# New tables of order, PSUM banks and engines for a fused attention and phase-mixer kernel

## The chip, the cores and the metric

The kernel runs on one core of one Trainium2 chip. The metric is the device time of one execution in microseconds (us), the median of several runs. A core has five engines with a queue each, and each runs its queue in order: PE (TensorE, matrix products), DVE (VectorE), ACT (ScalarE), POOL (GpSimd) and SP (SyncE, which here only issues DMA transfers). Work of one engine that needs another's waits on a semaphore, and everything behind it in that engine's queue waits too.

## The reference

```
def _attn_ref(q, k, v):                       # (8, 8, 576, 64) each
    scores = scale * np.matmul(q, k.transpose(0, 1, 3, 2))
    mask = block_i >= block_j                 # causal, in blocks of 64
    scores = np.where(mask, scores, -1000000000.0)
    attn = softmax(scores)
    return np.matmul(attn, v)

def _moe_ref(x, w_theta, w_tok_r, w_tok_i, w_ch):   # x: (8, 576, 512)
    theta = x @ w_theta
    zr, zi = x * np.cos(theta), x * np.sin(theta)
    y = einsum('ts,bsd->btd', w_tok_r, zr) + einsum('ts,bsd->btd', w_tok_i, zi)
    u = x + y
    return u + np.maximum(u @ w_ch, 0.0)

def reference(...):
    x = attention of all heads, laid out as (batch, 576, 512)
    return _moe_ref(x, ...)
```

Everything is float32. Eight batches of eight heads each go through attention; the result of a batch, 576 by 512, goes through the mixer.

## The kernel before

The work is cut into 3,404 **parts**, each a small function with a key, the parts that it needs, and where it matters a PSUM bank and an engine that are chosen for it. Heads are numbered 0 to 63 and handled in pairs 0 to 31; batch b has the pairs 4b to 4b + 3. Products in float32 accuracy are made of three float16 products (a high part times a high part and the two cross terms), which is why most tensors exist as a high and a low half.

A **pair** is loaded as `rq`, `rk`, `rv` in groups of two pairs (line 772). Its scores are made by PE into the two wide banks and two narrow ones (lines 589 and 596) and, for the first 64 rows, into a corner of the bank of the outputs (line 617). DVE takes row maxima (line 633), DVE or POOL turns them into the bias `mn` (line 641), ACT takes exponentials into `t` (line 646). The exponentials are split: the high half by a cast (`high`, line 431 on ACT, 433 on DVE or POOL), the low half by a subtraction (`low`, line 436, on DVE or POOL). SP transposes the halves by DMA (`pt<-p`, line 665), in two pieces A and B for heads below 16 and in one piece above. PE multiplies them with `v` (line 680, 45 products for a head), and DVE divides by the row sums (lines 692, 694, 698) into `xn`; a small DMA (line 686) moves one corner.

The **mixer** of a batch follows its four pairs: `xn` is split (`xh`, `xl`: lines 431/433 and 436) and transposed by DMA (`xT<-xp`, line 806); PE makes theta (lines 816 and 819), ACT and DVE make cosine and sine (828, 834, 440/442, 849, 851), DVE or POOL multiplies with x (`z`, line 860) and splits (`zh`, `zl`). PE mixes tokens with `wT` (line 884, five pieces for each of eight tiles: the **mix**), DVE makes u (893; `xs`, line 889, is the sum of x's halves), ACT/DVE/POOL splits u (423/425/427 and 900), PE mixes channels (907), ACT or DVE clips (913/915) and DVE adds up (923); SP stores (927).

The **weights** come in float64 words and are brought into two float16 halves in the first 110 us: a load (462), `exponent` on ACT (471), `lowest` (477 on ACT, 479 on POOL, 481 on DVE), `narrow` on DVE (485), `plain` (440 on ACT, 501 on DVE), a product with ones on PE for the largest size (494), `high` (423 on ACT, 425 on DVE, 427 on POOL) and `low` on DVE (507).

The scales of the values in `v` (and of q, k from the fourth batch on) also need a small product on PE (line 374) of a diagonal that POOL makes (368).

No scheduler runs when the kernel is built. What stands where is written in three **tables**: `ORDER` lists all parts in the order in which they are emitted, and so sets the order on every queue; `BANKS` gives one of the eight PSUM banks to each of 371 takings of a bank; `PLACES` gives one of A (ACT), D (DVE) and P (POOL) to each of 915 parts that could go to more than one engine. They are used in one function:

```
    keys, names, places, place = list(parts), iter(BANKS), iter(PLACES), {}
    for key in keys:
        for label in parts[key].takes:
            of_label[label] = banks[int(next(names))]
        if parts[key].on:
            place[key] = next(places, parts[key].on[0])
    done = set()
    for n in ORDER:
        key = keys[n]
        assert done.issuperset(parts[key].needs), key
        parts[key].f(*([place[key]] if parts[key].on else []))
        done.add(key)
```

Of the kernel before, what the change touches and what calls it, by code (L numbers as in the profile page):

```python
# [37 lines left out]
    8, 160, 158, 16, 9, 10, 11, 17, 18, 335, 363, 339, 364, 372, 373, 374, 340, 0, 1, 350, 351, 19, 12, 352, 353,  # L38
    375, 336, 387, 2, 334, 361, 3, 362, 365, 24, 337, 386, 32, 33, 25, 56, 338, 341, 392, 376, 342, 26, 57, 40, 58,
    41, 366, 367, 20, 27, 162, 42, 4, 343, 368, 5, 48, 59, 49, 28, 391, 390, 354, 50, 43, 163, 13, 344, 21, 29, 34,  # L40
    385, 51, 35, 369, 415, 164, 401, 60, 165, 414, 388, 345, 72, 413, 44, 104, 64, 136, 88, 96, 80, 161, 346, 347,
    105, 106, 402, 403, 412, 166, 416, 167, 168, 389, 36, 65, 73, 89, 97, 423, 169, 52, 74, 170, 171, 172, 159, 90,
    393, 66, 394, 98, 332, 81, 355, 82, 137, 107, 75, 348, 437, 395, 67, 37, 396, 397, 398, 138, 120, 424, 333, 99,
    112, 383, 45, 53, 349, 404, 377, 76, 83, 384, 139, 100, 356, 61, 14, 91, 417, 84, 418, 68, 92, 69, 357, 441, 77,
    358, 85, 425, 359, 93, 101, 465, 370, 141, 151, 466, 121, 122, 436, 113, 176, 142, 143, 178, 144, 94, 371, 114,
    115, 439, 419, 360, 78, 378, 420, 489, 440, 116, 22, 399, 438, 443, 62, 123, 6, 38, 494, 379, 464, 421, 442,
    444, 380, 173, 452, 447, 445, 434, 540, 463, 467, 446, 145, 15, 128, 140, 426, 427, 174, 381, 468, 469, 70, 405,
    406, 474, 152, 453, 108, 448, 30, 487, 31, 435, 470, 449, 454, 86, 455, 456, 180, 400, 124, 129, 130, 471, 491,
    490, 495, 407, 514, 408, 409, 410, 488, 382, 475, 428, 476, 477, 478, 545, 496, 1804, 492, 422, 450, 497, 493,
# [12 lines left out]
    650, 673, 631, 604, 669, 611, 693, 1854, 1869, 651, 670, 646, 1855, 645, 656, 657, 1864, 639, 612, 613, 698,
    614, 1857, 1865, 652, 678, 658, 632, 564, 691, 1862, 196, 1858, 1859, 692, 633, 586, 615, 1863, 626, 653, 679,
    680, 681, 694, 695, 689, 659, 699, 700, 660, 682, 654, 661, 696, 701, 1908, 697, 1909, 744, 634, 1866, 721, 674,
    702, 1910, 720, 197, 1899, 729, 1914, 1915, 730, 707, 718, 635, 1870, 191, 1867, 1916, 1900, 1873, 1901, 199,
    636, 1871, 683, 690, 703, 719, 708, 709, 1885, 637, 675, 710, 722, 200, 676, 2004, 2007, 1881, 201, 119, 655,
    662, 663, 664, 665, 711, 1911, 749, 1884, 704, 1912, 705, 712, 1880, 2005, 155, 1907, 731, 1877, 1902, 723, 684,
    1893, 1917, 724, 202, 1903, 1894, 1895, 725, 1888, 1872, 1896, 1897, 1918, 1892, 666, 1898, 1913, 677, 203,
    1904, 2008, 1889, 2006, 1882, 685, 1919, 743, 1890, 1876, 1878, 1886, 1879, 742, 686, 1874, 1875, 1905, 687,
    726, 727, 785, 195, 732, 747, 748, 745, 746, 750, 753, 204, 706, 713, 205, 1944, 765, 714, 715, 716, 754, 751,  # L70
    752, 755, 733, 1945, 756, 764, 767, 766, 157, 1938, 1887, 1883, 1939, 734, 1940, 206, 768, 688, 771, 1946, 2009,
    790, 757, 1941, 758, 772, 769, 1891, 770, 773, 193, 1947, 207, 135, 208, 1937, 192, 1948, 1949, 1942, 1943, 717,
    2010, 735, 728, 736, 737, 738, 740, 739, 741, 783, 784, 786, 826, 2023, 788, 787, 789, 791, 2024, 759, 808,
# [1103 lines left out]
```

## Time and profile before

| | us |
|---|---|
| median of three runs (673.57 to 674.95) | 674.0 |
| the profiled execution, its own time | 677.03 |
| its span, first instruction to last | 675.2 |
| PE busy | 614.8 |
| DVE busy | 586.5 |
| ACT busy | 508.3 |
| POOL busy | 374.3 |

The profile shows one execution. Its own time is 3.0 us over the median of the runs and 1.8 us over its span. Times inside it are counted from the start of the span. An engine is busy while an instruction runs on it; waiting and issuing don't count. Instructions that follow each other on one engine overlap a little at their ends, so the sum of durations is larger than the busy time.

### The profile page before, as it was taken

The page shows a single profiled execution, that of the slowest core. Times are in us where ns is not written, and L with a number is a line of the kernel's source. Part 1 is how long each engine was busy: PE and PEld are TensorE (multiplying, and loading weights), DVE is VectorE, ACT ScalarE, POOL GpSimd, SP SyncE. Part 2 cuts the span into 40 slices and gives each one's busy share as a digit, 9 for nine tenths or more (in the row PEclk, how much of TensorE's full clock was granted, in tenths as well). Part 3 has the DMA queues.
Part 4 walks back from the last instruction along what each step waited for, and adds up shares of the span by engine and source line. Part 5 has one row for each costly group of instructions (what it writes and reads, how often), then busy time and mean ns, then how long its engine had stood idle before and what let it go on. Part 6 is the DMA issues. An engine that isn't in the chain of part 4 may idle for free.

```text
span 675.2 us, 18061 instructions
## 1 busy us (share of the span) xinstructions
PE 614.8 (91%) x7374; PEld 456.1 (68%) x7374; DVE 586.5 (87%) x1162; ACT 508.3 (75%) x770; POOL 374.3 (55%) x391
## 2 busy tenths in 40 slices
PE   5376688998999999999999998999899999999997
PEld 3155545785688577775787756785677477867775
DVE  3988889998997999989998899999998999976554
ACT  5888669885987998877998799979987997225021
POOL 2463536853667467961677628744593457931530
PEclk9577788999999999999999999999999999999999
DMA  8999999899969688879789977999779547930003
GB/s 349 336 264 224 196 196 225 183 202 187 202 141 237 132 190 188 183 157 185 202 178 154 206 168 169 199 165 213 169 177 184 93 81 161 189 78 2 19 1 123
DMA packets 268515, 116.58 MB, mean 173 GB/s; under 512 B 256016, under 2 KB 256016, under 8 KB 268432
## 3 DMA queue, kind: packets, MB, share of 16 engines
q1 hardware_dynamic: 268432, 115.43, 79.1%
q8 instruction: 57, 0.93, 0.6%
q14 instruction: 26, 0.21, 0.1%
HBM read 42.01 MB, written 9.44 MB: 76 GB/s over the span
## 4 chain that ended last, share of the span: by engine, by line
PE 52%; DVE 22%; DMA 10%; ACT 8%; POOL 4%; issue 4%; SPq 1%; ACTq 0%; POOLq 0%; DVEq 0%
PE g L884 12%; PE s L884 8%; DMA pt<-p 7%; PE g L680 7%; DVE m L633 5%; PE g L816 5%; PE g L907 5%; PE s L589 4%; PE s L907 4%; DVE p L436 3%; PE s L816 3%; ACT t L646 3%; PE g L589 2%; DMA xT<-xp 2%; PE s L819 1%
## 5 line engine op out<-in xcount | busy, mean ns | idle before, releaser
L884 PEld LDWEIGHTS <-zh 128*128 128x128 f16 x1152 | 112.7, 98 | 29.8 <-issue 1.1
L884 PE MATMUL g<-wT_h,zh 128*128 128x288 f16 x405 | 115.9, 286 | 1.0 <-DVE u L893 0.8
L884 PE MATMUL g<-wT_h,zl 128*128 128x288 f16 x405 | 115.8, 286 | 0.1
L884 PE MATMUL g<-wT_l,zh 128*128 128x288 f16 x405 | 115.8, 286 | 0.0
L680 PE MATMUL g<-v,pt 128*128 128x65 f16 x2880 | 102.9, 197 | 13.3 <-DMA pt<-p 6.5
L680 PEld LDWEIGHTS <-pt 128*128 128x128 f16 x2880 | 99.0, 100 | 20.3 <-DMA pt<-p 10.3
L633 DVE TENSOR_REDUCE m<-s 128x1 f32<-128x576 f32 (+2 forms) x132 | 85.3, 672 | 6.9 <-PE s L596 6.9
L436 POOL TENSOR_TENSOR p<-t,p 128x512 f16<-128x512 f32 (+4 forms) x28 | 66.5, 2376 | 43.8 <-ACT p L431 38.9
L431 ACT CAST p<-t 128x1600 f16<-128x1600 f32 (+4 forms) x66 | 84.3, 1283 | 8.5 <-DMA pt<-p 4.4
L436 DVE TENSOR_TENSOR p<-t,p 128x1600 f16<-128x1600 f32 (+4 forms) x52 | 84.9, 1635 | 5.0 <-ACT p L431 3.5
L860 POOL TENSOR_TENSOR aa<-aa,xn 128x256 f32<-128x256 f32 (+1 forms) x59 | 48.3, 832 | 60.3 <-ACT aa L849 44.4
L816 PEld LDWEIGHTS <-xT 128*128 128x128 f16 x384 | 36.6, 99 | 46.9 <-DMA xT<-xp 4.3
L884 PEld LDWEIGHTS <-zl 128*128 128x128 f16 x576 | 56.3, 98 | 16.3 <-issue 1.6
L646 ACT ACTIVATE t<-s,m,size 128x576 f32<-128x576 f32 (+1 forms) x80 | 59.1, 778 | 7.8 <-POOL m L641 6.5
L907 PEld LDWEIGHTS <-wch_h 128*128 128x128 f16 x512 | 48.1, 98 | 15.8 <-issue 2.8
L633 DVE TENSOR_REDUCE m<-g 128x1 f32<-128x192 f32 (+2 forms) x156 | 54.4, 372 | 4.5 <-PE g L596 4.4
L646 ACT ACTIVATE t<-g,m,size 128x320 f32<-128x320 f32 (+2 forms) x100 | 49.0, 535 | 11.9 <-DVE m L641 5.7
L436 POOL TENSOR_TENSOR zl<-aa,zh 128x512 f16<-128x512 f32 (+1 forms) x36 | 40.8, 1139 | 15.3 <-ACT zh L431 9.5
L884 PE MATMUL s<-wT_h,zh 128*128 128x288 f16 x171 | 48.9, 286 | 0.0
L884 PE MATMUL s<-wT_l,zh 128*128 128x288 f16 x171 | 48.9, 286 | 0.0
L884 PE MATMUL s<-wT_h,zl 128*128 128x288 f16 x171 | 48.9, 286 | 0.0
L907 PE MATMUL g<-uh,wch_h 128*128 128x288 f16 x160 | 45.8, 286 | 1.4 <-DVE u L893 0.8
(194 smaller groups left out, 1624.3 us busy)
## 6 DMA issues: line engine op xcount, KB each, us to landing
rv<-in_v SPq DMA_DIRECT2D x16, 768.0 KB, 5.4
rq<-in_q SPq DMA_DIRECT2D x16, 640.0 KB, 5.1
rk<-in_k SPq DMA_DIRECT2D x16, 576.0 KB, 5.0
out<-xT SPq DMA_DIRECT2D x32, 288.0 KB, 2.8
w_raw<-in_w_tok SPq DMA_DIRECT2D x5, 576.0 KB, 6.7
pt<-in_w_tok SPq DMA_DIRECT2D x4, 576.0 KB, 8.5
w_raw<-in_w_theta SPq DMA_DIRECT2D x4, 512.0 KB, 7.0
w_raw<-in_w_ch SPq DMA_DIRECT2D x4, 512.0 KB, 4.7
```

The source lines that it names most:

```text
L431: nc.scalar.copy(out=out, in_=x)
L436: engine_of(on).tensor_tensor(out=out, in0=x, in1=y, op=ALU.subtract)
L589: nc.tensor.matmul(to[hh][:, col:col + n], lhsT=qq[rows, P + P * i:P + P * i + P], rhs=kk[rows, k0:k0 + n], start=nn == 0 and col % 512 == ...
L633: nc.vector.tensor_reduce(out=self.m[:, i:i + 1], in_=self.scores_of(i), axis=AX.X, op=ALU.max)
L646: nc.scalar.activation(out=t_parts[self.hh][:, to:to + n], in_=self.scores_of(i), func=AF.Exp, scale=self.scales()[0], bias=self.m[:, NI + ...
L680: nc.tensor.matmul(o[:, i, :], lhsT=source[:, block, :], rhs=vv[:, slot, hh, :], start=first, stop=last)
L816: nc.tensor.matmul(g, lhsT=xT[:, xx + i, :], rhs=ww[:, dt, :], start=first, stop=last)
L819: nc.tensor.matmul(g[half * D:half * D + D, 0:HC], lhsT=xT[:, xx + i, 0:D], rhs=ww[:, dt, half * HC:half * HC + HC], start=first, stop=last)
L860: engine_of(on).tensor_tensor(out=cd, in0=cd, in1=self.xns[dt][:, i0:i0 + ni, :], op=ALU.mult)
L884: nc.tensor.matmul(g, lhsT=zz[:, kk, cols], rhs=ww[:, kk, ts], start=(n == 0 and kk == k0 and nn == 0), stop=n == 4 and kk == k0 + ni - 1 ...
L907: nc.tensor.matmul(g[:, 0:HS], lhsT=ww[:, dt, e * P:(e + 1) * P], rhs=uu[:, dt, th * HS:(th + 1) * HS], start=dt == 0 and n == 0, stop=dt ...
```

## The change

The parts, what each does and what it needs are the same. The three tables are replaced: they were searched with ten sets of durations of the parts, and are now searched anew with twelve. 3,300 of the 3,404 places of `ORDER` hold another number, mostly since the parts around them moved by some places; 153 of 371 letters of `BANKS` and 341 of 915 of `PLACES` differ. D falls from 279 to 266, A rises from 289 to 296, P from 347 to 353.

```diff
 ORDER = [
-    8, 160, 158, 16, 9, 10, 11, 17, 18, 335, 363, 339, 364, 372, 373, 374, 340, 0, 1, 350, 351, 19, 12, 352, 353,
...
+    8, 9, 158, 10, 11, 160, 336, 335, 363, 364, 340, 339, 16, 17, 18, 19, 350, 341, 0, 1, 2, 3, 32, 33, 351, 334,
...
```

By kind, the parts that changed engines count, before and after:

| part | ACT | DVE | POOL |
|---|---|---|---|
| steps of the weights (lowest, plain, high) | 24, 31 | 15, 6 | 12, 14 |
| low half of exponentials | - | 52, 57 | 28, 23 |
| high half of exponentials | 66, 65 | 4, 7 | 10, 8 |
| high half of v | 24, 16 | 4, 3 | 4, 13 |
| z, the products with x | - | 57, 49 | 103, 111 |
| zh | 43, 53 | 11, 6 | 26, 21 |
| xs, the sum of x's halves | - | 17, 13 | 15, 19 |
| high half of k | 11, 15 | 3, 2 | 6, 3 |

Three places follow. Names are those of the buffers: `p0` and `p1` (in the second and third place `p_99` and `p_100`) hold the split exponentials of the first and the second head of a pair, `t_97` and `t_98` the exponentials, `s_` and `g_` are PSUM banks, `pt` is the transposed `p`.

The first place is the queue of SP some 25 us after the start, before:

```order
L462 DMA w_raw_127<-in_w_tok 128x1152
L462 DMA pt01_106<-in_w_tok 128x1152
L772 DMA rk_287<-in_k 128x1152
L772 DMA rq_314<-in_q 128x1280
L665 DMA_TRANSPOSE pt00_104<-p0_99 128x8x128
L665 DMA_TRANSPOSE pt00_104<-p0_99 128x18x128
L462 DMA w_raw_128<-in_w_ch 128x1024
```

And after:

```order
L462 DMA w_raw_127<-in_w_tok 128x1152
L462 DMA pt11_107<-in_w_tok 128x1152
L665 DMA_TRANSPOSE pt00_104<-p0_99 128x8x128
L772 DMA rq_292<-in_q 128x1280
L772 DMA rk_294<-in_k 128x1152
L665 DMA_TRANSPOSE pt00_104<-p0_99 128x18x128
L462 DMA w_raw_128<-in_w_ch 128x1024
```

The first transposition of head 0 moved ahead of the loads of q and k of the second two pairs.

The second place is the queue of DVE between the first maxima and the largest size of the theta weights, before:

```order
L436 TENSOR_TENSOR p_100<-t_98,p_100 128x1024
L633 TENSOR_REDUCE m<-g_113 128x1
L641 TENSOR_SCALAR m<-m 128x2
L501 TENSOR_SCALAR wT_h<-w_val 128x576
L633 TENSOR_REDUCE m<-g_113 128x1
L633 TENSOR_REDUCE m<-s_109 128x1
L633 TENSOR_REDUCE m<-s_110 128x1
L501 TENSOR_SCALAR wT_h<-w_val 128x576
L518 TENSOR_REDUCE size_theta<-g_112 128x1
```

And after:

```order
L433 CAST p_99<-t_97 128x1088
L436 TENSOR_TENSOR p_99<-t_97,p_99 128x1088
L633 TENSOR_REDUCE m<-s_110 128x1 x2
L726 TENSOR_REDUCE size<-size 128x1
L633 TENSOR_REDUCE m<-s_109 128x1 x2
L641 TENSOR_SCALAR m<-m 128x3
L641 TENSOR_SCALAR m<-m 128x2
L485 SCALAR_TENSOR_TENSOR w_val<-w_val,w_raw 128x576
L436 TENSOR_TENSOR p_100<-t_98,p_100 128x512
L518 TENSOR_REDUCE size_theta<-g_113 128x1
```

The `plain` steps of the token weights (line 501) left DVE here and went to ACT (line 440), and both halves of head 0's larger piece came to DVE.

The third place is the queue of POOL where the low halves of the heads 18 and 19 stood, before:

```order
L427 TENSOR_SCALAR v_87<-rv,size 128x12x64
L889 TENSOR_TENSOR u_2219<-xT 128x576
L436 TENSOR_TENSOR p_99<-t_97,p_99 128x1600
L433 CAST p_100<-t_98 128x1536
L436 TENSOR_TENSOR p_100<-t_98,p_100 128x1536
L860 TENSOR_TENSOR aa<-aa,xn 128x2x128
L641 TENSOR_SCALAR m<-m 128x5
```

And after, the queue of DVE at the same heads:

```order
L900 SCALAR_TENSOR_TENSOR ul<-u_1980,u_scales,uh 128x576
L633 TENSOR_REDUCE m<-g_113 128x1 x2
L633 TENSOR_REDUCE m<-g_111 128x1
L433 CAST p_100<-t_98 128x1536
L436 TENSOR_TENSOR p_100<-t_98,p_100 128x1536
L633 TENSOR_REDUCE m<-s_109 128x1
L860 TENSOR_TENSOR aa<-aa,xn 128x2x128
```

Head 19's high and low half went from POOL to DVE, as did the low halves of the heads 18 and 23; POOL got products `z` and sums `xs` of DVE's in exchange.

## Rows read from the trace of the kernel before

**Rows 1.** The page: busy us (share of the span) and instructions of each engine.

```profile
PE 614.8 (91%) x7374; PEld 456.1 (68%) x7374; DVE 586.5 (87%) x1162; ACT 508.3 (75%) x770; POOL 374.3 (55%) x391
```

**Rows 2.** Busy time by stretch: PE, PEld, DVE, ACT, POOL; granted clock, DMA, GB/s.

```profile
0.00:125.00 125.00, 84.40 (x913) 58.58 (x914) 103.77 (x223) 96.98 (x159) 59.02 (x90) 0.81 1.01 249
125.00:550.00 425.00, 409.21 (x5231) 303.84 (x5228) 394.04 (x779) 366.12 (x546) 260.42 (x253) 1.00 0.87 177
550.00:675.20 125.20, 121.20 (x1245) 93.63 (x1238) 88.70 (x162) 45.25 (x68) 54.82 (x50) 1.00 0.36 81
125.00:225.00 100.00, 97.24 (x1225) 75.00 (x1222) 89.43 (x190) 79.78 (x128) 64.59 (x61) 1.00 0.99 196
```

**Rows 3.** Whom PE waited for: us in total, times, longest us.

```profile
PE g L589 <- DMA rq<-in_q: 10.7, 2, 7.6
PE g L680 <- DMA pt<-p: 6.5, 6, 2.2
PE g L680 <- DVE xn L698: 3.8, 4, 1.4
```

**Rows 4.** The page's chain that ended last, share of the span by engine.

```profile
PE 52%; DVE 22%; DMA 10%; ACT 8%; POOL 4%; issue 4%; SPq 1%; ACTq 0%; POOLq 0%; DVEq 0%
```

**Rows 5.** Groups by form: count, busy us, mean ns of one, idle before them.

```profile
L436 DVE TENSOR_TENSOR p<-t,p 128x1536 f16<-128x1536 f32 x13 | 24.3, 1868 | 1.8 <-ACT p L431 1.8
L436 DVE TENSOR_TENSOR p<-t,p 128x512 f16<-128x512 f32 x5 | 3.6, 713 | 2.0 <-POOL p L433 1.3 <-ACT p L431 0.7
L436 DVE TENSOR_TENSOR xp<-xn,xp 128x640 f16<-128x640 f32 x13 | 10.7, 819 | 1.6 <-ACT xp L431 1.4
L436 DVE TENSOR_TENSOR zl<-rr,zh 128x512 f16<-128x512 f32 x11 | 9.4, 854 | 0.0
L860 DVE TENSOR_TENSOR rr<-rr,xn 128x256 f32<-128x256 f32 x20 | 10.2, 512 | 0.0
L889 DVE TENSOR_TENSOR u<-xT 128x576 f32<-128x576 f16 x17 | 18.3, 1075 | 0.1
L436 POOL TENSOR_TENSOR p<-t,p 128x1536 f16<-128x1536 f32 x11 | 36.6, 3328 | 21.6 <-ACT p L431 18.2 <-DVE r L692 2.9
L433 DVE CAST zh<-aa 128x256 f16<-128x256 f32 x3 | 2.6, 870 | 0.0
L481 DVE TENSOR_SCALAR w_raw<-w_raw 128x576 uint32<-128x576 uint32 x2 | 1.0, 488 | 0.0
L501 DVE TENSOR_SCALAR wT_h<-w_val 128x576 uint16<-128x576 uint16 x4 | 1.7, 446 | 0.0
L440 ACT ACTIVATE wT_h<-w_val 128x576 bf16<-128x576 f32 x5 | 3.3, 682 | 0.0
```

**Rows 6.** Order of time, SP, PE and DVE before 40 us: start us, us, what.

```profile
26.44 0.70 SPq L772 DMA_DIRECT2D rq<-in_q  x1
27.18 9.86 SPq L665 DMA_TRANSPOSE pt<-p  x2
...
36.32 2.18 PE L589 MATMUL g<-rk,rq 64*128 64x320 f32 x12 [3.17 <-DMA rq<-in_q]
...
26.57 1.94 DVE L641 TENSOR_SCALAR m<-m 128x2 f32<-128x2 f32 x1
```

**Rows 7.** Order of time, PE: products of the heads 15, 23, 44 and 50 begin.

```profile
154.76 1.43 PE L680 MATMUL g<-v,pt 128*128 128x65 f16 x41 [1.87 <-DMA pt<-p]
223.25 0.94 PE L680 MATMUL g<-v,pt 128*128 128x65 f16 x25 [0.29 <-DMA pt<-p]
425.48 1.20 PE L680 MATMUL g<-v,pt 128*128 128x65 f16 x34 [1.32 <-DMA pt<-p]
483.19 0.97 PE L680 MATMUL g<-v,pt 128*128 128x65 f16 x27 [1.37 <-DVE xn L698]
```

**Rows 8.** All instructions of a line: duration ns min/median/max, first and last start.

```profile
L860 POOL TENSOR_TENSOR rr<-rr,xn x44: 720/732/2240, 116.0 to 639.6; 128x256 f32<-128x256 f32 x44
L900 DVE SCALAR_TENSOR_TENSOR ul<-u,u_scales,uh x32: 804/812/3524, 168.4 to 660.9; 128x576 f16<-128x576 f32 x32
```

More of the change, by code (lines that the diff above doesn't have):

```diff
@@ L37 @@
 ORDER = [
[176 rows of a table removed]
[176 rows of a table added]
 ]
 BANKS = (
-    "5064556406401235601234601235401235601234501230101236401236501234601236501235601235401235601235401236501236501234"
-    "6012356012345012364012356012346012364012345012365012354012364012356012356012354012365012345256416041444565640601"
-    "5460114565666400654160425114445344454666166240165566554506655104502141064066556041425110660526466456611400541625"
-    "63463210534066451601352025430645142"
+    "6640455415101234601234501235401235401236501230101236401235601234601236501236401236501234601234501235401234501234"
@@ L220 @@
+    "5012356012354012364012346012346012345012356012356012364012356012364012346012354012365012356246515041550565440441"
+    "5460560214666650466150524616666244541656064530665500455604466101503640144155446541520126505646466544456100451342"
+    "31315450463621054620463501434154206"
 )
 PLACES = (
-    "DAAPDAADPDDPAAAADDDADADAAAPDAPPDAPDPPAAPADAAPAAPADAADAPPADPPDPDPAPPPDAPPADDPDADADDPPDADPPPAPADDPDPAPPAPAPDDDAPPA"
-    "DPAPADAPPAPPADPPDDDADPADPADPAPPDADPAPPADPAPPPADDADPDAPDPPDPADDADAPADPAPADADADDAPAAADADPAPDAAPADPADPPAPADPADAPADA"
@@ L224 @@
-    "DPADAPADDDDAPAAADADDAPPDDPADDADAPADAPDADAPAPADPADAAADADPPDPAAPADPADAAAPADPADAPAPADPADAAPPADDAPPAADADDADAAAPDDDAP"
-    "AAADADPAPAADPADDPPPDAPADPAPADAPADAPAADAAPPPPPPAPPPAPDPADDDAPDDAPPDAPDDAPDPADPPAPDADPPPDAAAADDAAAADAPAPDDAAAAADPP"
-    "PDPPPDDAPDPAPDPPPDDPPDDAPPPADPPADPDADDADAPAPDADADADAAAPAPAPDDAAADADDPPPPAPPDPPPPDPPPAPPPAPDPAPDPAPPPPDPPDPDPDAPP"
-    "PPAAAAADAAPPAPADDDDADAAPPPPDDPPDDPPDDPDPPAPPPAPPPAPPPAPPPAPPPADPAPADPDADAADDAADADPPPPPPAADADPPAPPDPPPPAPPPPDPPPP"
-    "DPAPPDAPPDADPDPDPPAPPADAPPDADAADADADAPADAPPPAADDAPPPDDPAPPPPPDPADDPPPDDAPPPAPDPAPPPDPPPAPPAPDPADAAADDADDAPPADAPA"
@@ L229 @@
-    "DAAADAPPADDPPPPDPPPPDPPPPPDDDPPPPDDDPDPDPPDDADDAPDDADDDAAADDADPPADAPDDDAADDDDDDPDPPDDDDPPDPPDDDPPAPPPADPPDDPPADP"
-    "PDPPADADPPADADAADAD"
+    "ADAAAAADPPAPAADPAAPAAPAAPAAADAADPAAAPAAADPPAPAAPAAPADDDPPDDPPPPDPDADPADDADPDDPDADPAPDAPDDPDPADPAPDAPDAPAPADPAPPA"
+    "DPPDADAPPAPPADPPDDPADPADPADPAPAPADPADDADPAPAPADDADPDADDDDPDADDADADADDADAADPADDAPAAPPADDAPAAAPADDADPPAPADPADAPADA"
+    "PPADAAAPDDPAPAAADADPAPPDPDADDADAAAPAPPADADPDPDPADAAPDADPPDPAAPADDADAAPDADDADAAPPADPPDAAPPADPAPAAAPADDADAAAPADDDP"
@@ new lines @@
+    "AAAPDDDAPAAPPAPPAPPPPPADPADDDAPADAPADDAAPDDDPPAPPPAPPDADPPDPDDAPDPADDDAPPPADPPAPPADPPDDAAAAAADADADADAPDPAAAAAPDP"
+    "PPDAPPPAPPPAPPPDDDPAPDDPDDPAPPPADPPPPPADAPAPAADDDAADAPDADAPDDDAAAAPPAPDPAPDPADDDAPPPPPDDAPPPADDPAPPDAPPPPPPPPAPP"
+    "PDDAAAADAAPPPDAPDDADADDPPAPPDAPPDPPDPAPPPAPPDAPPPAPDDPPPPADPDAPPAPPDPDADAAADDADAPAPAPAPAADDDPPADPPPPPPAPDPAPPPAP"
+    "DPAPPPAPDPAPPDADPPAPPPDADPPADDDDADADAPADAPAPAADDDPDPPPPAPPPPPDPAPPPPPPPAPDDADPPAPPPAPDPAPDADPDDPAAAADAAAAPDADDPA"
+    "DAAADAPPADPDADPPADPDADPDPPPPPDPDPPPDDPPPPPPPPPPAPADAPDADDAADADPDDPPPADDDADADPPDDDDPPPAPPPPDDPPPPPPDPPPPDDDPPDAPP"
@@ L231 @@
+    "PADPDDAPADPDADDAAAA"
 )
```

350 rows, old and new, of the table ORDER are left out of this document.

## The prediction

> **What bounds the kernel now.** I read the page's busy times first, then the busy times by stretch, then whom PE waited for, then the chain that ended last. PE is busy 614.8 us of 675.2 [rows 1], so some 60 us are idle, and the stretches say where: 125.00 − 84.40 = 40.6 us before 125, 425.00 − 409.21 = 15.8 us from 125 to 550, and 125.20 − 121.20 = 4.0 us after that [rows 2]. The reader is to see two limits. After 125 PE leaves almost nothing free, and since the matrix products are the same parts in both kernels, the tables can win there no more than parts of the 15.8 us. Before 125 PE waits for data: its largest waits of all are for the loads of q (10.7 us) [rows 3]. The chain that ended last agrees: PE 52%, DVE 22%, DMA 10%, ACT 8%, POOL 4% [rows 4]; the shares that are not PE's lie mostly in the opening. After 125 PE waits for transposed exponentials (6.5 us in 6 waits) and for `xn`, by which DVE frees the bank of the outputs (3.8 us in 4) [rows 3]; the heads 15, 44 and 50 have most of that, 1.87 + 1.32 + 1.37 = 4.56 us [rows 7]. DVE comes next. From 125 to 225 it is busy 89.43 of 100 us, so 10.6 us are idle, while ACT has 20.2 and POOL 35.4 us idle there [rows 2]. So an edit counts if it delays or hastens what DVE or a transposition hands to PE before 550, or shortens the opening.
>
> **The change part by part.** Everything but order, banks and engines is the same, so nothing is added or removed in total; what counts is how much work stands in a queue ahead of a point at which PE waits.
>
> *The loads and the first transposition.* SP issued the q of the second two pairs at 26.44 and then the transposition of head 0 at 27.18, which kept SP 9.86 us for its two pieces [rows 6]. After the change the first piece stands ahead of both loads. In the row PE waits 3.17 us for that q, up to 36.32 [rows 6]. If the loads are issued later by one issue or two (0.70 us each), the scores of the second two pairs come 0.7 to 1.4 us later; if the transfers only share the engines in another order, nothing changes. I take +0.0 and keep +1.0 for the range, since PE has other idle time in the opening that can take it up (40.6 us in all).
>
> *DVE ahead of the first mix.* Weight steps leave: four `lowest` at 0.488, three `plain` at 0.446 [rows 5], and two `high` at about 0.5 (the row of `plain` is the nearest), 1.95 + 1.34 + 1.0 = 4.3 us. In their place come two low pieces at 0.713 (1.43), a `zl` at 0.854 [rows 5] and some five short ones (a half of v, of x, of z, a high piece, a size) at 0.4 to 0.6, 2.5 us: together 4.8, and a few products `z` (0.512 each [rows 5]) move out again. The sum is about zero. One thing may not recur: the bias step at 26.57 took 1.94 us [rows 6], where another short step of DVE takes 0.446 [rows 5], and that piece of the queue is rearranged; it is worth 1.5 us. So the opening's balance lies between 0 and −2.0, and I take **−1.0**, the middle, as no row is nearer to one end.
>
> *DVE ahead of the product of head 23.* Here DVE gets work from POOL: three low halves at 1.87 (5.60), three low pieces at 0.713 (2.14), two `xl` at 0.819 (1.64), two `zl` at 0.854 (1.71), two `zh` of half size at 0.870 (1.74) [rows 5], and eight shorter steps, half of them at the 0.446 of the smallest and half at some 0.66, between 0.446 and 0.870 [rows 5], 4.4 us: 17.2 us. It loses two `xs` at 1.075 (2.15), seven `z` at 0.512 (3.58) [rows 5], the 4.3 us of weights and a half of k (0.5): 10.5 us. Net **+6.7 us** of durations; with the eight short ones all at one end or the other, and means instead of the rows for the rest, 4.6 to 9.3. Of this the opening's balance is already a part. It must go into the 10.6 us that DVE idles between 125 and 225 [rows 2]. I take it that it fits, at no cost, because these steps have a long way to go before PE needs them: the low half of a head on POOL lasts 3.33 us, on DVE 1.87 [rows 5], so each of the three comes out sooner even if it begins 1.4 us later. The cover is those 10.6 us; without it the cost is up to 6.7.
>
> Whether two engines hinder each other matters for these prices. The products `z` on POOL take 0.732 us in the middle and up to 2.240, and `ul` on DVE 0.812 and up to 3.524 [rows 8]: the same work, so something else delays it. The Trainium skill, page "SBUF — State Buffer", section "Who interferes with whom", says that a VectorE instruction with two inputs from SBUF and a GpSimd instruction that uses SBUF exclude each other for the whole instruction, first come first served. The rows fit that. It speaks against the change mildly: eleven such instructions are added to DVE ahead of head 23 and nine leave it. By the rule the net two cost at most 2 × (2.240 − 0.732) = 3.0 us [rows 8], so +6.7 would be up to +9.7; by the rows alone it stays +6.7.
>
> *POOL and ACT.* POOL gives up the three low halves (3 × 3.33 = 10.0 us [rows 5]) and smaller things and gets `z` and `xs`, and has 35.4 us idle anyway [rows 2]. Nothing waits longer for POOL; the price is zero, and the gain, if any, is the second rival's. ACT gets three `plain` at 0.682 [rows 5], 2.0 us, two `lowest` and two `high` of about the same length each, 2.9 us, and loses small ones, about 0.8: **+4.1 us**, into 20.2 us of idle time [rows 2]; I take it at nothing.
>
> *After 225.* DVE's share falls slightly until the end (fewer `z` and `xs`), but after 550 PE is idle only 4.0 us [rows 2], so relief there is worth nothing. PE's own order is moved by single places only.
>
> The sum: 0.0 (loads) − 1.0 (opening) + 0.0 (DVE under its idle time) + 0.0 (POOL, ACT) = −1.0 us. The profiled execution took 677.03 with a span of 675.2; 1.0 us off gives a span of 674.2. The median of the runs is 674.0, 3.0 below the profiled execution, and the difference is carried over as it is: **673.0 us**.
>
> **The rivals.**
>
> *DVE becomes the one that is late (slower).* The place is the product of head 23, which began at 223.25 after a wait of only 0.29 us for its transposition [rows 7]. DVE's idle time comes in small pieces behind PE and ACT, and a queue in order can use only those pieces behind which the next step is ready. If a quarter of the 10.6 us is usable (2.7), 6.7 − 2.7 = 4.0 us remain, and PE has nothing else to do at that place, as its 2.8 us of idle time in these 100 us show [rows 2]. 674.0 − 1.0 + 4.0 = **677.0 us**; with nothing usable 679.7. It decides from the point where head 23 starts later than 223.25 − 1.0. For it: DVE is the second busiest engine, at 89% there. Against it: the low halves come sooner than on POOL.
>
> *PE's waits for the transpositions shrink (faster by more).* If POOL's relief and the shorter low halves bring the transposed exponentials earlier, half to all of the 4.56 us at the heads 15, 44 and 50 [rows 7] go: 673.0 − 2.3 = 670.7 to 673.0 − 4.6 = 668.4; at two thirds, **670.0 us**. For it: the order stands otherwise, and those waits are the ones that a new order can take away. Against it: each wait removed tends to be followed by the next at the same bank.
>
> *ACT becomes late.* The 4.1 us that ACT gets stand ahead of head 23 too. If they delay the exponentials there rather than fill idle time, 673.0 + 4.1 = **677.1 us**. Against it: 20.2 us idle [rows 2].
>
> *The tables do nothing that counts.* The opening's 1.0 us is given back by the q behind the transposition (+1.0), and nothing else is on the path: **674.0 us**.
>
> **How the numbers follow.** The forecast, 673.0, has a chance of 0.38; of it I count 0.15 as faster by over 0.2% and 0.23 as within, since its own band, from the 0 to −2.0 of the opening and half a microsecond to either side, is 671.5 to 674.5 and the bound lies at 672.65. 0.2% is 1.35 us, about what a measurement of this kernel can tell from no change. PE's waits shrinking has 0.23 (faster), DVE late 0.24 and ACT late 0.08 (slower), nothing 0.07 (the same). Together: faster 0.15 + 0.23 = 0.38, the same 0.23 + 0.07 = 0.30, slower 0.24 + 0.08 = 0.32. The range reaches from 669.0, within the second rival, to 678.0, a little above the middle value of the slower ones; the ends that are left out (668.4 and 679.7) hold about 2 in 10 of the chance. By sign the forecast is not sure; alone, the likeliest case lies in 671.5 to 674.5.
>
> **What would show each step.** Right: PE's busy time before 125 about 1 us higher or the first mix about 1 us earlier (it starts near 125 now), the bias step of DVE near 26 us at half a microsecond, the wait for the second q near 36 us unchanged, DVE's idle time from 125 to 225 down from 10.6 to some 4 us, and the product of head 23 begun by 222 with a wait under 0.5 us. The slower rival shows as waits of PE for `pt<-p` between 175 and 225 of some 4 us, with the low halves of the heads 18, 19 or 23 late on DVE; the faster one as PE idle from 125 to 550 of 11 to 13 us instead of 15.8, with the rows of the heads 15, 44 and 50 free of their waits. The ACT rival shows as DVE's waits for casts and PE's for exponentials. The prediction is wrong if PE's idle time before 125 moves by over 2 us either way, or if waits appear after 225, where I count nothing.

## The result and the profile after

The changed kernel takes 667.84 us (median of four runs, 666.52 to 669.22) against 674.34 for the kernel before: a ratio of 0.990 (95% interval 0.988 to 0.992). It is 6.5 us faster; forecast were 1.0 us, with 669.0 as the lower end of the range. Measured twice more beside other kernels, it stood at 0.9891 and 0.9900. The profiled execution has a span of 665.5 us and a time of 667.24.

The page of the changed kernel, busy us and instructions, answers to [rows 1]:

```profile
PE 611.8 (92%) x7372; PEld 455.0 (68%) x7374; DVE 583.9 (88%) x1149; ACT 508.4 (76%) x777; POOL 380.9 (57%) x397
```

PE is idle 665.5 − 611.8 = 53.7 us instead of 60.4, and busy 3.0 us less with the same products; the granted clock of the opening is higher, as the next rows show. The busy times by stretch (PE, PEld, DVE, ACT, POOL, granted clock, share of the DMA engines, GB/s) answer to [rows 2]:

```profile
0.00:125.00 125.00, 88.69 (x954) 61.63 (x957) 109.36 (x232) 104.67 (x173) 66.54 (x95) 0.85 1.05 257
125.00:550.00 425.00, 411.91 (x5311) 307.54 (x5309) 401.05 (x787) 364.60 (x545) 254.91 (x244) 1.00 0.85 177
550.00:665.50 115.50, 111.21 (x1112) 85.83 (x1109) 73.54 (x132) 39.13 (x61) 59.48 (x60) 0.99 0.37 79
125.00:225.00 100.00, 97.89 (x1205) 73.23 (x1203) 95.20 (x195) 78.27 (x125) 49.44 (x51) 1.00 0.91 189
```

PE's idle time before 125 went from 40.6 to 36.3 us and the mean clock there from 0.81 to 0.85; from 125 to 550 the idle time went from 15.8 to 13.1, and behind that it stayed (4.3 against 4.0). The prediction had named a move of over 2 us before 125 as a sign that it is wrong; it moved by 4.3. DVE's idle time from 125 to 225 went from 10.6 to 4.8 us, where some 4 were forecast. Whom PE waited for (us in total, times, longest) answers to [rows 3]:

```profile
PE g L617 <- DMA rk<-in_k: 7.4, 1, 7.4
PE g L680 <- DMA pt<-p: 5.1, 8, 1.8
PE g L680 <- DVE xn L698: 4.7, 5, 1.4
```

The second wait for the first loads (3.17 us at 36.32 [rows 6]) is no longer among them. The products of the heads 15, 23, 44 and 50, in order of time, answer to [rows 7]:

```profile
149.07 1.54 PE L680 MATMUL g<-v,pt 128*128 128x65 f16 x45
...
217.84 1.34 PE L680 MATMUL g<-v,pt 128*128 128x65 f16 x38
...
417.40 1.53 PE L680 MATMUL g<-v,pt 128*128 128x65 f16 x45 [0.99 <-DMA pt<-p]
...
476.65 1.51 PE L680 MATMUL g<-v,pt 128*128 128x65 f16 x45 [1.39 <-DVE xn L698]
```

Head 23 begins 5.4 us earlier and waits for nothing, so DVE is not late there. Head 15's wait of 1.87 us is gone, head 44's is 0.99 instead of 1.32, head 50's stays. This pair of executions puts most of the lead ahead of 223 us, but the profiled execution of the kernel before was 3 us longer than its median. In the second traces below (e1 and e9) head 23 begins at 221.02 and 219.47, only 1.5 us apart. So the opening, where 1.0 us was expected, is the first place to look, and the time after 225, where nothing was, is as good a place.

### The profile page after: what moved, and what is told of

Read it like the earlier page. It is cut to its first block, busy times and chain, and to the rows that moved or that the text cites. A ratio compares the mean times of both kernels' runs of the same rounds, so it can differ in the third digit from the quotient of the medians.

```text
span 665.5 us, 18051 instructions
## 1 busy us (share of the span) xinstructions
PE 611.8 (92%) x7372; PEld 455.0 (68%) x7374; DVE 583.9 (88%) x1149; ACT 508.4 (76%) x777; POOL 380.9 (57%) x397
## 5 line engine op out<-in xcount | busy, mean ns | idle before, releaser
L884 PE MATMUL g<-wT_h,zh 128*128 128x288 f16 x369 | 105.8, 287 | 0.6 <-ACT t L646 0.6
L884 PE MATMUL g<-wT_h,zl 128*128 128x288 f16 x369 | 105.7, 287 | 0.1
L884 PE MATMUL g<-wT_l,zh 128*128 128x288 f16 x369 | 105.7, 287 | 0.0
L436 DVE TENSOR_TENSOR p<-t,p 128x1600 f16<-128x1600 f32 (+4 forms) x57 | 91.7, 1610 | 1.9 <-ACT p L431 1.8
L431 ACT CAST p<-t 128x1536 f16<-128x1536 f32 (+4 forms) x65 | 82.2, 1273 | 3.1 <-DMA pt<-p 2.1
L436 POOL TENSOR_TENSOR p<-t,p 128x512 f16<-128x512 f32 (+4 forms) x23 | 53.8, 2345 | 35.8 <-ACT p L431 25.0
L816 PEld LDWEIGHTS <-xT 128*128 128x128 f16 x384 | 36.3, 98 | 45.7 <-issue 3.5
L884 PE MATMUL s<-wT_h,zh 128*128 128x288 f16 x207 | 59.3, 287 | 0.0
L884 PE MATMUL s<-wT_l,zh 128*128 128x288 f16 x207 | 59.3, 287 | 0.0
L884 PE MATMUL s<-wT_h,zl 128*128 128x288 f16 x207 | 59.3, 286 | 0.0
L633 DVE TENSOR_REDUCE m<-g 128x1 f32<-128x320 f32 (+2 forms) x156 | 54.2, 371 | 4.2 <-PE g L596 4.0
```

Source lines behind the costliest of these rows:

```text
L431: nc.scalar.copy(out=out, in_=x)
L436: engine_of(on).tensor_tensor(out=out, in0=x, in1=y, op=ALU.subtract)
L633: nc.vector.tensor_reduce(out=self.m[:, i:i + 1], in_=self.scores_of(i), axis=AX.X, op=ALU.max)
L816: nc.tensor.matmul(g, lhsT=xT[:, xx + i, :], rhs=ww[:, dt, :], start=first, stop=last)
L884: nc.tensor.matmul(g, lhsT=zz[:, kk, cols], rhs=ww[:, kk, ts], start=(n == 0 and kk == k0 and nn == 0), stop=n == 4 and kk == k0 + ni - 1 ...
```

## The experiments

Times are medians of several rounds against the kernel before on the same chip; the intervals are 95%. Start times in the opening differ between single executions by up to 3.5 us with the same parts in the same queues: with the old opening unchanged, the first mix starts at 124.94 (before), 124.84 (e1), 124.40 (e10), 124.13 (e14), 122.82 (e8), 122.59 (e15) and 121.41 us (e3), 123.6 on average. So no single start time decides anything here; the times do, and waits that are compared with several traces. A graft is a table whose first part comes from one kernel and whose rest from the other; `order_b` and `order_a` are the orders of before and after, and each part takes its bank and its engine from the table that its place in the order is from.

**The kernel before again (e1).** No edit.

> The kernel before, unchanged, with a second profile. If its profiled execution (677.03 us against a median of 674.0) was slow by something in the opening that does not recur, the first mix starts 2 to 3 us earlier than 124.9 here and the bias step of DVE near 26 us takes about 0.5 us, not 1.94; if the excess lies elsewhere, the first mix starts within 1 us of 124.9. The time is the same as before (ratio 0.998 to 1.002).

Measured: ratio 0.999 (0.996 to 1.002), span 674.1 us. The bias step that took 1.94 us takes 1.94 again, and the first mix starts at 124.84. The step is no accident of one execution. It is not what made the profiled execution 3 us longer than the median.

**The opening of after, then before (e2), and the reverse (e3).**

```diff
-ORDER = order_b
+ORDER = order_a[:597] + [n for n in order_b if n not in order_a[:597]]     # e2
+ORDER = order_b[:600] + [n for n in order_a if n not in order_b[:600]]     # e3
```

> The new tables up to the first mix (597 of 3,404 parts), the old ones for all parts behind. Theory A (the gain was made in the opening, where my prediction allowed 0 to 2.0 us): 5 us faster than before, 669 us, ratio 0.992. Theory B (the gain comes from shorter waits of PE after 125 us, my second rival): 1 us faster, 673 us, ratio 0.998.

> The old tables up to the first mix (600 parts), the new ones for all parts behind. Theory A: 1.5 us faster than before, 672.5 us, ratio 0.998. Theory B: 5.5 us faster, 668.5 us, ratio 0.992.

Measured: e2 1.005 (1.002 to 1.008), e3 0.997 (0.995 to 0.999). Neither theory said that, and neither run tells them apart, because the seam costs. In e2 the mix starts, and then PE stands still at the seam (lines of this kernel are 5 lower: 879 is the mix, 641 the exponentials):

```profile
135.94 0.40 PE L879 MATMUL g<-wT_h,zh 128*128 128x288 f16 x1 [3.60 <-ACT t L641]
```

In e3 the seam shows a wait of 2.37 us at 138.54. So these two runs are inconclusive for the sum. But e3 has the old opening up to the mix, and yet its mix starts 3.4 us before that of e1:

```profile
121.41 0.29 PE L879 MATMUL g<-wT_h,zh 128*128 128x288 f16 x1
```

**One load later in the old tables (e4).** The queues of SP in the two traces show a difference that the prediction had not looked at: in the old order the load of q for the pairs 6 and 7 stands between the first and the second transposition of x. First the unchanged kernel (e1), then the changed one, SP's queue in order of time:

```profile
84.65 1.36 SPq L806 DMA_TRANSPOSE xT<-xp  x1
86.07 0.69 SPq L772 DMA_DIRECT2D rq<-in_q  x1
86.88 1.36 SPq L806 DMA_TRANSPOSE xT<-xp  x1
```

```profile
81.42 1.43 SPq L806 DMA_TRANSPOSE xT<-xp  x1
83.38 0.46 SPq L686 DMA_DIRECT2D xn<-xn  x1
83.95 1.27 SPq L806 DMA_TRANSPOSE xT<-xp  x1
...
98.25 0.57 SPq L772 DMA_DIRECT2D rq<-in_q  x1
```

In the chain of the kernel before, which the prediction read by engine only [rows 4], the same place reads so (start us, us, what; traced back from 98 us):

```profile
85.67 0.67 SPq L772
...
86.45 6.14 DMA xT<-xp
...
92.64 4.27 PE g L816 x12
```

In this execution the load, the transposition behind it and the products of theta hang on one another, and PE waits 2.36 us. In e1, the same kernel, the transposition takes longer still (6.5 us), but PE comes late itself and waits 0.45 us, and its chain goes by another way:

```profile
92.64 0.60 PE L816 MATMUL g<-wth_h,xT 128*128 128x512 f16 x2 [2.36 <-DMA xT<-xp]
93.40 0.60 PE L816 MATMUL g<-wth_h,xT 128*128 128x512 f16 x2 [0.45 <-DMA xT<-xp]
```

The edit in SP's queue:

```diff
 L806 DMA_TRANSPOSE xT<-xp 128x10x128
-L772 DMA rq<-in_q 128x1280
 L806 DMA_TRANSPOSE xT<-xp 128x10x128
...
 L665 DMA_TRANSPOSE pt_105<-p_100 128x8x128
+L772 DMA rq<-in_q 128x1280
 L772 DMA rk<-in_k 128x1152
```

> The kernel before with one DMA moved in SP's queue: the load of q for the pairs 6 and 7 goes from ahead of the second transposition of x (85.7 us) to behind the last transposition of head 9 (101 us), where the new tables have it too. Theory A1 (this load held up the transfers behind it, since the second x transposition landed 5 us after the first, against 3.2 us in the changed kernel, and the corner transfer of head 6 at 92.8 against 85.6): 2 to 3 us faster than before, 671.5 us, PE's wait of 2.36 us for the transposed x near 92.6 is gone. Theory A2 (the load is hidden; the opening is shorter through the weights' steps): within 0.5 us of before.

Measured: 0.998 (0.996 to 1.001), 1.1 us, not clear of zero. The transposition itself shows an effect: from issue to landing (us, last number) it takes 6.5 in e1, 3.4 in e4 and 4.5 in the changed kernel, in this order:

```profile
xT<-xp SPq DMA_TRANSPOSE x1, 6.5
```

```profile
xT<-xp SPq DMA_TRANSPOSE x1, 3.4
```

```profile
xT<-xp SPq DMA_TRANSPOSE x1, 4.5
```

PE does not wait for it in e4. The first mix starts at 122.08 us, 2.8 earlier than in e1, but that lies within the spread of the unchanged opening (121.41 to 124.94).

**The same load put back in the new tables (e5).** The edit in SP's queue is the reverse, ahead of the transposition at 83.95.

> The changed kernel with one DMA put back: the load of q for the pairs 6 and 7 stands ahead of the second transposition of x again, as in the old tables. Theory A1 (this load delayed the transposed x of batch 0 and with it the first mix): the second transposition of x lands 2 to 4 us later than 88.4 us, PE waits there again, and the kernel is 2 us slower than the changed one, about 0.993 of before. Theory A2 (other parts of the opening made the gain): as the changed kernel, 0.990.

Measured: 0.9958 (0.9935 to 0.9982), while the changed kernel has 0.9898, 0.9891 and 0.9900. By the times this one place costs 4 us, some 2 to 6 by the two intervals (each ratio is taken on its own chip). The transposition takes 5.8 us, but PE waits for it only 0.38:

```profile
93.34 0.60 PE L816 MATMUL g<-wth_h,xT 128*128 128x512 f16 x2 [0.38 <-DMA xT<-xp]
```

The first mix starts at 124.19, and in three traces of the changed kernel at 119.72, 121.35 and 122.34. That difference is not the load's: SP's queue is the same up to the load, which is issued at 86.46 us, and e5's execution was 4.3 us behind the first of these traces before that. First the changed kernel, then e5, the same product, and after it the busy times from 70 to 90 us:

```profile
77.59 0.22 PE L374 MATMUL g<-diag,ones 128*128 128x128 bf16 x1 [1.91 <-POOL diag L368]
81.88 0.26 PE L374 MATMUL g<-diag,ones 128*128 128x128 bf16 x1 [1.41 <-POOL diag L368]
```

```profile
70.00:90.00 20.00, 13.97 (x185) 9.68 (x187) 16.60 (x43) 16.12 (x26) 11.73 (x13) 0.91 1.05 192
70.00:90.00 20.00, 16.05 (x163) 11.97 (x163) 13.88 (x35) 14.60 (x25) 11.77 (x13) 0.53 0.84 174
```

PE was granted 0.53 of the clock there, almost all of it the lower level (1.2 GHz), where the changed kernel had 0.91, and over the whole span it was busy 618.2 us against 611.8, with no more idle time (52.8 against 53.7 us). So the ten times of e5 show that the place of the load counts, and by how much; by which way it does is not shown by its trace. The granted clock is one candidate: its mean over the executions is 0.965 in e5 and 0.970 in the changed kernel. It can't be all of it, since e18 below has 0.965 too and is as fast as the changed kernel.

What the rest of the new tables ahead of head 46 is worth without the load is best read from times: e5 has 0.9958, and e10 below, with the old tables there, 0.9959.

**The engines of the weights' steps (e6).** 30 letters of the table of engines, for example the `lowest` of two weights:

```diff
-place["w", 0, 2], place["w", 3, 2] = "D", "D"
+place["w", 0, 2], place["w", 3, 2] = "A", "P"
```

> The kernel before with the engines of the weights' steps alone taken from the new tables (30 letters: lowest, plain and high), in the old order. Theory A2 (lowest off DVE frees the raw buffers earlier, so that the later weights and the loads behind them are fetched sooner): the loads of the weights 6, 9 and 10 are issued at about 13, 16 and 17 us as in the changed kernel, not at 16.5, 20.6 and 25.3, and the kernel is 1 to 2 us faster, 0.998. Theory B (my prediction: these steps are worth their durations, minus at most 2.0): between 0 and 1.0 us faster, loads issued where they were. If the old order doesn't suit these engines, it is slower by up to 2 us.

Measured: 1.000 (0.998 to 1.002). The loads of the weights 6, 9 and 10 are issued at 16.27, 19.90 and 25.85 us: the engines alone don't free the raw buffers earlier. Theory A2 falls.

**The first transposition ahead of two loads (e7).**

```diff
-L772 DMA rk_287<-in_k 128x1152
-L772 DMA rq_314<-in_q 128x1280
 L665 DMA_TRANSPOSE pt00_104<-p0_99 128x8x128
+L772 DMA rq_314<-in_q 128x1280
+L772 DMA rk_287<-in_k 128x1152
```

> The kernel before with the loads of q and k for the pairs 2 and 3 moved behind the first transposition of head 0 in SP's queue, as the new tables have it, and nothing else. My prediction: 0.0 with up to 1.0 us slower, since these loads are issued later. Theory A3: in the changed kernel they land 3 us sooner, at 33 us, since the transposition is not held behind them; then 1 us faster here. Both differ little in time; the landing of q (36.2 before) tells them apart.

Measured: 1.0005 (0.998 to 1.003). q lands at 35.3 and k at 36.7, against 36.2 and 34.5 before; both are needed, so 0.5 us later. The prediction's first step (0.0, at most 1.0) holds; A3 falls.

**Three low halves on DVE (e8).**

```diff
-place["low", 18, "all"], place["low", 19, "all"], place["low", 23, "all"] = "P", "P", "P"
+place["low", 18, "all"], place["low", 19, "all"], place["low", 23, "all"] = "D", "D", "D"
```

> The kernel before with the low halves of the heads 18, 19 and 23 on DVE instead of POOL, and nothing else. My forecast: DVE takes the 5.6 us into its idle time between 125 and 225 and the time is the same as before (0.999 to 1.001), DVE's idle time there down by 4 to 6 us. The slower rival: the product of head 23 late by 3 us, 1.004.

Measured: 1.001 (0.999 to 1.003). From 125 to 225, e1 and then e8:

```profile
125.00:225.00 100.00, 99.32 (x1232) 75.82 (x1229) 91.23 (x195) 80.88 (x129) 65.92 (x61) 1.00 0.97 196
```

```profile
125.00:225.00 100.00, 97.35 (x1214) 74.30 (x1212) 92.44 (x194) 78.77 (x126) 53.91 (x56) 1.00 0.94 192
```

POOL is relieved of 12.0 us, and the time is the same: DVE has the room for these three steps. DVE's idle time in this window is down by only 1.2 us, where 4 to 6 were expected, and its busy time over the whole span is 592.8 instead of 588.6; its four steps `ul` there (line 900) take 4.0 us in all instead of 6.5. For these three steps the forecast's cover is confirmed and the slower rival falls; the other steps that came to DVE were not tried.

**The last third (e10, e11), with the changed kernel as a control (e9).**

```diff
-ORDER = order_b
+ORDER = order_b[:2317] + [n for n in order_a if n not in order_b[:2317]]     # e10
+ORDER = order_a[:2308] + [n for n in order_b if n not in order_a[:2308]]     # e11
```

> The changed kernel again, with a second profile, as a control beside the three others: 0.990 of before (0.988 to 0.992). Its second trace tells which leads over before recur: if the opening's lead is real, the first mix starts again by 121 us.

> The old tables up to the product of head 46 (2,317 parts, 441 us), the new ones behind. Theory L (some 3 us of the gain come from the stretch 480 to 570, where PE's waits are fewer): 2.5 to 3.5 us faster than before, 0.9955. Theory O (all the gain that counts is from the opening): within 0.5 us of before, 1.000.

> The new tables up to the product of head 46 (2,308 parts), the old ones behind. Theory L: 3.5 to 4 us faster than before, 0.9945. Theory O: as the changed kernel, 0.990.

Measured: e9 0.9891 (0.9855 to 0.9927), first mix at 121.35; e10 0.9959 (0.9938 to 0.9980); e11 0.9967 (0.9942 to 0.9991). So 2.8 us come from the tables behind the product of head 46 alone, and 2.2 from what stands ahead of it, the moved load included; Theory L holds. The two add up to 5.0 of 6.8 us, and the rest lies within the intervals. Whom PE waited for, e1 from 455 to 600 (the first six of 13 rows) and e10 from 456 to 596 (all rows):

```profile
PE g L680 <- DVE xn L698: 1.4, 1, 1.4
PE g L680 <- DVE m L633: 0.9, 1, 0.9
PE g L589 <- DVE rr L834: 0.9, 1, 0.9
PE g L374 <- POOL diag L368: 0.8, 1, 0.8
PE g L589 <- DVE xT L923: 0.6, 1, 0.6
PE s L907 <- ACT t L646: 0.6, 1, 0.6
```

```profile
PE g L680 <- DVE xn L698: 2.0, 2, 1.4
PE g L589 <- DVE u L893: 0.9, 1, 0.9
PE g L884 <- ACT t L646: 0.6, 1, 0.6
PE s L374 <- POOL diag L368: 0.5, 1, 0.5
PE g L816 <- ACT t L646: 0.4, 1, 0.4
```

All 13 rows of e1 add up to 8.0 us, those of e10 to 4.4, and e9 has the five rows of e10 word for word in its own stretch. Thirteen waits of 0.2 to 1.4 us became six, 3.6 us less in all. PE has almost no other idle time there (8.0 us by its busy time in e1, 4.5 in e10), so nearly all of it counts: by the times 2.8 us.

**Order without engines (e14), engines without order (e15),** both for the last third only.

```diff
 # e14: the order and banks of e10
-place = place of after behind the cut
+place = place of before
 # e15: the order and banks of before
-place = place of before
+place = place of after behind the cut
```

> The old tables up to the product of head 46, the new order and banks behind, with the old engines everywhere (124 letters of the last third put back). If the order makes the late gain: 0.995 to 0.997 of before, and the six waits of PE that went stay away. If the engines make it: 1.000 or slower.

> The kernel before with the new engines behind the product of head 46 (124 letters) in the old order. If the engines make the late gain: 0.995 to 0.997 of before. If the order makes it: 1.000, or slower where the old order doesn't suit them.

Measured: 1.0415 (1.039 to 1.044) and 1.0415 (1.039 to 1.044): 28 us slower, either way. In e14 PE idles 25.4 us from 441 to 600, against 7.0 in the kernel before, in many waits of up to 2.9 us. So neither table is an improvement that could be had alone. The 124 letters and the 1,087 places were searched for each other; that this is the reason is argued, not shown.

**The load and the last third together (e13), with the changed kernel on the same chip (e16).** The edits of e4 and e10.

> The old tables with the one load moved (as in the run of the late load), and the new tables behind the product of head 46. Theory P (two pieces make the whole change: the place of one load, and the last third of the order): 0.990 to 0.993 of before, near the changed kernel. Theory Q (the rest of the new opening and middle is worth 2 us or more of its own): 0.994 to 0.996, clearly above the changed kernel.

> The changed kernel once more, on the same chip as the three others, to compare the two pieces with the whole: 0.990 (0.988 to 0.992).

Measured: e13 0.9946 (0.993 to 0.996), e16 0.9900 (0.988 to 0.992). Two pieces are not the whole: 3.1 us are missing, and the intervals don't meet. The trace of e13 has a wait of 1.94 us at the second transposition of head 15, which stands in SP's queue behind a load of q again, this time of the pairs 10 and 11:

```profile
144.54 0.65 SPq L772 DMA_DIRECT2D rq<-in_q  x1
145.29 1.23 SPq L665 DMA_TRANSPOSE pt<-p  x1
```

That transposition takes 7.2 us from issue to landing; in the changed kernel, where the load was issued 4.4 us ahead of it, it takes 4.0. This is the wait of 1.87 us of [rows 7]. It is no fixed price: in e1 and e4, with that load at the same place, the transposition took 4.9 us and PE did not wait.

**A second load moved too (e17), and seven loads in the changed kernel (e18).** e17 is e13 with the load of the pairs 10 and 11 behind that transposition:

```diff
-L772 DMA rq<-in_q 128x1280
 L665 DMA_TRANSPOSE pt<-p
+L772 DMA rq<-in_q 128x1280
 L686 DMA xn<-xn 64x64
```

> The old tables with two loads moved in SP's queue, and the new tables behind the product of head 46: the load of q for the pairs 6 and 7 as in the run of the late load, and the load of q for the pairs 10 and 11 from ahead of the second transposition of head 15 to behind it. In the run with one load and the late part, that transposition took 7.2 us from issue to landing behind that load and PE waited 1.94 us for it, which ate what the first load had won. Theory P (such loads and the last third make the whole change): that wait goes, 0.990 to 0.9925 of before, 2 us faster than with one load. Theory Q (the rest of the new opening and middle counts by itself): 0.994 to 0.995, as with one load.

Measured: 0.9926 (0.990 to 0.995). The transposition takes 3.3 us and PE's wait at head 15 is gone, but the 1.4 us against e13 are within the intervals. By the time, it lies between Theory P and Theory Q, and its interval covers both: that the two loads and the last third are the whole change is not shown.

e18 moves seven loads in the changed kernel in the same manner, each behind a transposition or a corner transfer that is waited for.

```diff
-L772 DMA rv<-in_v 128x1536
 L686 DMA xn<-xn 64x64
 L665 DMA_TRANSPOSE pt_107<-p_100 128x8x128
 L686 DMA xn<-xn 64x64
 L665 DMA_TRANSPOSE pt_104<-p_99 128x18x128
 L665 DMA_TRANSPOSE pt_104<-p_99 128x8x128
+L772 DMA rv<-in_v 128x1536
...
```

> The changed kernel with seven loads moved behind the transposition or corner transfer that stands next to them in SP's queue and that PE, ACT or DVE waits for (v of batch 1; q and k of batch 2; q of batch 5; v of batch 6; q of batch 7). By the trace of the changed kernel these loads land 5 to 29 us before they are used, and the transfers behind them are waited for at once. If loads ahead of transpositions are what costs, 1 to 3 us faster than the changed kernel, 0.985 to 0.988 of before; if those waits are covered by others (DVE, ACT), within 0.5 us of the changed kernel, 0.990.

Measured: 0.9891 (0.986 to 0.993), as the changed kernel. Its profiled span of 664.5 is the shortest of all, but the times don't tell it from 665.5 to 666.9. So loads ahead of such transfers cost nothing that can be measured at these seven places; under which waits they lie was not looked at.

**The loads between the transpositions of head 9 (e12).** In the changed kernel:

```diff
+L772 DMA rq<-in_q 128x1280
+L772 DMA rk<-in_k 128x1152
 L665 DMA_TRANSPOSE pt_105<-p_100 128x8x128
-L772 DMA rq<-in_q 128x1280
-L772 DMA rk<-in_k 128x1152
```

> The changed kernel with the loads of q and k for the pairs 6 and 7 one place earlier in SP's queue, between the two transpositions of head 9 instead of behind both. In the changed kernel PE waits 1.3 us for this k at 105 us; if that wait is on the path, it goes and the kernel is 0.5 to 1.5 us faster than the changed one (0.988); if the second transposition of head 9 then comes late, the same or slower (0.990 to 0.992).

Measured: 0.9915 (0.988 to 0.995), the same within the interval. PE's wait for k at 105 us is gone, and in its place it waits 1.49 us for the transposition, as the second expectation had it. No version was found that beats the changed kernel by more than the measurement tells.

## Why the prediction was wrong

*What bounds the kernel.* Right in outline (PE nearly full after 125, data before), but the sentence that the shares of the chain that are not PE's lie mostly in the opening was read no further. The chain's own pieces at 85.67, 86.45 and 92.64 us, shown above, name the load and the transposition, in that execution. And the heads 15, 44 and 50 have 4.56 of the 10.3 us that PE waits for transposed exponentials and for `xn` [rows 3], less than half and not most.

*The loads and the first transposition, 0.0 with at most +1.0.* Right for the edit it speaks of (e7). The failed step is that it was the only place of SP's queue that was looked at. The table moved every load, and one of them, issued at 98 us instead of 86 and so behind the transposed x of batch 0, is worth 4 us in the new tables (e5) by the times; how it comes to that much, with 0.38 us of wait for the transposition, stays open. The sign that was named, an unchanged wait for q near 36 us, did not come either: in the changed kernel q has landed by 33.05 us. What brought that forward is not shown; e6 and e7 alone don't do it. The rule was at hand: each queue past which a step is moved has to be gone through, SP's too, over its whole length.

*DVE ahead of the first mix, −1.0.* The size was not measured: the first mix starts at 121.2 us on average in five traces of the new opening (after, e2, e9, e11, e16) and at 123.6 in the seven of the old one, 2.4 us earlier, but that holds the load's share too. The times put the new tables ahead of head 46 without the load at nothing (e5 against e10). The reason was partly wrong. The bias step of 1.94 us is indeed gone, as the changed kernel's DVE shows, but the low half of head 0 took its place, 3.10 us:

```profile
25.48 3.10 DVE L436 TENSOR_TENSOR p<-t,p 128x1088 f16<-128x1088 f32 x1
...
31.07 0.24 DVE L641 TENSOR_SCALAR m<-m 128x3 f32<-128x3 f32 x2
```

*DVE ahead of head 23, +6.7 us that fit into 10.6.* Nothing speaks against it: 4.8 us idle are left, head 23 waits for nothing, and e8, with three of the steps alone, is 1.001. The weights, the sums and the products that moved the other way were not tried one by one.

*POOL and ACT at nothing.* Nothing in the waits of the changed kernel speaks against it from 125 to 225, where ACT still has 21.7 us idle; not tried alone.

*After 225, nothing.* Wrong, by about 2.8 us (e10), and this is the failed step that is shown best. The paragraph argues from the 4.0 us behind 550 and passes over the 15.8 − 2.8 = 13.0 us that PE idles between 225 and 550 [rows 2]. That PE's own order is moved by single places only proves nothing, since the waits there are of 0.2 to 1.4 us, each for one step of another engine. Of the 15.8 us between 125 and 550 the prediction priced three waits, 4.56 us, as a rival, and left the rest as it is. Behind 550, where 4.0 us were idle, nothing changed, as forecast.

*The second rival* named the right kind of gain, waits of PE that go, and its lower end (668.4) is near the measured 667.84, but the reasons were not its own. Of its 4.56 us, 1.87 + 0.33 = 2.2 went, and the larger part not by shorter low halves: where head 15 waits, its transposition stands behind a load of q (e13, e17), and in e1 it doesn't wait at all. So the nearness of the number is in part luck. The other rivals, all slower or unchanged, fell with the measured time; for DVE at head 23 the trace and e8 say the same.

*The sum, as far as it is known.* Of some 6.8 us, the tables behind head 46 make 2.8 (e10), and the load ahead of the transposed x makes about 4 where the rest is new (e5). But the load makes only 1 where the rest is old (e4: 1.1, not clear of zero; e13 against e10: 0.9), and the rest of the tables ahead of head 46 makes nothing without the load (e5 against e10) and 3.1 us with it (e16 against e13). So these two count together and not one by one. Why is not shown. A wait at head 15 ate the load's lead in the trace of e13, but e4 has no such wait and is not faster by its time than e13 is against e10. With that wait removed as well (e17) the ratio is 0.9926 against 0.990 of the whole; the last 2 us or so, within the interval, stay open.

## What to carry to other kernels

Where one queue issues all transfers, list the large loads that stand just ahead of a transfer that an engine waits for, and try each by a run: here one such place was worth 4 us in the new tables, about 1 in the old ones, and seven others nothing (e18). On an engine that is 97% busy, add up its short waits by stretch instead of pricing the few long ones. Before a start time is read as a gain, look whether the lead was there ahead of the edit, and how far the start moves between executions of one and the same queue: here 3.5 us, more than most of the effects.

## What the runs showed of the hardware

A load delays what is issued behind it on the same queue, even a small transfer. The corner transfer of 16 KB behind the two transpositions of x, from issue to landing: 5.3 us in e1, where the load of 640 KB stands ahead of the second one, 2.2 us in e4, where only that load is moved away. The rows (size, us to landing), e1 and then e4:

```profile
xn<-xn SPq DMA_DIRECT2D x1, 16.0 KB, 5.3
```

```profile
xn<-xn SPq DMA_DIRECT2D x1, 16.0 KB, 2.2
```

The Trainium skill, page "DMA: Bandwidth & Descriptors", section "Queues, rings and completion order", says that each DMA engine takes the descriptors of a queue's ring in order; the traces agree with it, with these 5.3 against 2.2 us.

A pause of PE can cost more than its own length. After the wait of 3.60 us in e2, the granted clock was 0.50 for the next 4 us, the lower of its two levels (1.2 instead of 2.4 GHz), and 0.79 in the 4 us behind; before it PE had run at 1.00:

```profile
122.00:132.00 10.00, 10.00 (x123) 8.16 (x122) 9.64 (x21) 6.46 (x12) 8.12 (x9) 1.00 0.89 196
132.00:136.00 4.00, 0.40 (x13) 0.31 (x10) 3.43 (x8) 2.51 (x5) 0.12 (x1) 0.85 1.12 276
136.00:140.00 4.00, 4.00 (x18) 2.49 (x18) 0.77 (x2) 2.09 (x3) 3.39 (x4) 0.50 0.97 183
140.00:144.00 4.00, 4.00 (x40) 3.00 (x39) 0.61 (x2) 0.30 (x1) 0.00 (x0) 0.79 0.43 82
```

By these rows the products lose, as an estimate, 4 × 0.50 + 4 × 0.21 = 2.8 us beside the 3.6. The clock shows in PE's busy time of whole runs too: PE is busy 3.0 us less in the changed kernel, with the clock before 125 us at 0.85, than in the kernel before, with 0.81, and 6.4 us more in e5, with its 0.53 from 70 to 90 us, than in the changed kernel.
